# Float32 products of two head pairs in quarters of the array, from the ninth pair on

## The chip, the cores and the metric

One Trainium2 chip, one of its cores. The metric is device time of one execution in microseconds (us), the median of three runs. TensorE is called PE below, its weight loads PEld, VectorE DVE, ScalarE ACT, GpSimdE POOL, and SyncE, which only issues DMAs here, SP.

## The reference

Linear attention on 8 batches of 8 heads (576 tokens, 64 values each), followed by a two-layer MLP on 4608 tokens.

```python
q_s = np.exp(q - np.max(q, axis=-1, keepdims=True))
q_s = q_s / (np.sum(q_s, axis=-1, keepdims=True) + 1e-09)
k_s = np.exp(k - np.max(k, axis=2, keepdims=True))
k_s = k_s / (np.sum(k_s, axis=2, keepdims=True) + 1e-09)
kv = np.einsum('bhsd,bhse->bhde', k_s, v)
attn = np.einsum('bhsd,bhde->bhse', q_s, kv)
x = attn.transpose(0, 2, 1, 3).reshape(4608, 512)
h = x @ w_in                                  # 512 x 2048
g = h * np.tanh(np.log1p(np.exp(h)))          # Mish
out = g @ w_out                               # 2048 x 512
```

All is float32.

## The kernel before

The MLP's matrices are each split into two float32r parts, high and low, and each product is the sum of three float32r matmuls (high by high, high by low, low by high). The tokens go in chunks of 512 (the main part of a batch), and the last 64 tokens of each batch are gathered by way of DRAM (`xt_dram`) into a ninth chunk. A chunk has 16 steps, one for each 128 columns of the hidden layer. A step's `h_mm` makes `ph` from the attention output `xs` (12 matmuls of 512 columns), `act` applies Mish on ACT (`y`) and splits the result on DVE into `gh` and `gl`, and `out_mm`, three steps later, adds it into the four `po` (12 matmuls again). `ph` has two PSUM buffers (`ps_h`), `px` and the other small products two more (`ps_a`), `po` four.

The attention is worked off in the shadow of the MLP, one pair of heads at a time. There are 32 pairs, called items in the code, four for a chunk. Items 0 to 7 and the conversion of the weights stand in a list of tokens written out by hand (`FIRST`); from item 8 (`COLS`) on, `group` writes four MLP steps (`u` = 0 to 3) and puts the steps of one item between them. The order on each engine is the order of these calls. For an item of the later kind:

- k comes transposed (`kt`) for its maxima (`a_kmx`, DVE) and as it is for `a_ksub` (DVE) and the exponential `ke` (`a_exp`, ACT); q likewise: `a_qm` (DVE and POOL), `qe` (ACT), its sums `qs` and `a_qmul` (DVE, POOL), and `a_qt`, which transposes it on DVE into `qT` (512 tokens) and `qTt` (64).
- `a_kv` (step u = 1) multiplies `ke` by v, ten float32 matmuls of 66 columns: the two heads each in one half of the array's columns, five blocks of tokens each. A column of ones in v gives the sums of `ke`.
- `a_ksum` and `a_kvs` (DVE) divide by the sums and write both heads onto the diagonal of `kvbd`, of which two float32r parts `kvr` are made.
- `a_x` (u = 2) multiplies `kvr` by the parts of `qT`: three float32r matmuls of 512 columns in the whole array, into `px`. `a_split` makes the two parts of `xs` from it (ACT and DVE).
- `a_tail1` does the same for the 64 last tokens with one float32 matmul, `pxt`; it stands a group later, right ahead of the next item's `a_kv`. ACT copies it to `xt`, and SP sends it to `xt_dram`.

Of the kernel before, what the change touches and what calls it, by code (L numbers as in the profile page):

```python
# [48 lines left out]
def attn_mish_mlp(ctx: ExitStack, tc: tile.TileContext, q, k, v, wu, qs, kt, out):  # L49
# [39 lines left out]
    kvr = [cp.tile([P, P], F32R, tag=f"kvr{x}", name=f"kvr{x}") for x in "hl"]  # L89
    wi = [cp.tile([P, HP, DFF], F32R, tag=f"wi{x}", name=f"wi{x}") for x in "hl"]  # L90


# [73 lines left out]
    def k_load(i):  # L166
        if i >= NITEM:
            return
        r = at[i] = at.get(i, {})
        t = r["k"] = (pp if i < 3 else lp).tile([P, 2, NC + 1, D], F32, tag=f"k{min(i, 3)}", name=f"k{i}")  # L170
        nc.sync.dma_start(t, k[i])

    def q_load(i):
        if i >= NITEM:
            return
        r = at[i] = at.get(i, {})
        if i >= COLS:
            t = r["q"] = lp.tile([P, NB, 32], F32, tag="q3", name=f"q{i}")
            nc.sync.dma_start(t, qs[i].rearrange("p (n f) -> p n f", f=32))
            t = r["kt"] = lp.tile([P, S], F32, tag="kt", name=f"kt{i}")  # L180
            nc.sync.dma_start(t, kt[i])
# [4 lines left out]
    def a_load(i):  # L186
        q_load(i)
        k_load(i)

    def v_load(i):  # L190
        if i >= NITEM:
            return
        t = at[i]["v"] = vt[min(i, 3)]
        nc.sync.dma_start(t[:, :, :, 0:D], v[i])

    def a_kmx(i):
# [80 lines left out]
    def a_exp(i, which="kq"):  # L277
        if i >= NITEM:
            return
        r = at[i]  # L280
        for nm in which:
            if nm == "q" and i >= COLS:
                e = r["qe"] = ap.tile([P, NB, 32], F32, tag="qe", name=f"qe{i}")
                nc.scalar.activation(e, r["q"], AF.Exp)
                continue
            e = (pp if i in (0, 2) else ap).tile([P, NC + 1, 2, D], F32, tag=f"{nm}e", name=f"{nm}e{i}")
            nc.scalar.activation(e.rearrange("p c h d -> p h c d"), r[nm], AF.Exp)  # L287
            r[nm + "e"] = e

    def a_kv(i):  # L290
        if i >= NITEM:
            return
        r = at[i]
        pkv = psum(i, "o0", f"pkv{i}")
        for c in range(NC + 1):
            if i >= COLS:
                for j in range(2):
                    nc.tensor.matmul(pkv[j * D:(j + 1) * D, 0:D + 2], r["ke"][:, c, j],  # L298
                                     r["v"][:, j, c, :], start=c == 0, stop=c == NC)
            else:  # L300
                nc.tensor.matmul(pkv[:, 0:2 * (D + 2)], r["ke"][:, c].rearrange("p h d -> p (h d)"),
                             r["v"][:, :, c, :], start=c == 0, stop=c == NC)
        r["pkv"] = pkv

# [23 lines left out]
    def a_kvs(i, on_act=False):  # L328
        pkv, rs = at[i]["pkv"], at[i]["rs"]
        bd = kvbd[i in (1, 3) or i >= HP]  # L330
        for j in range(2):
            h = slice(j * D, (j + 1) * D)
            o = 0 if i >= COLS else j * (D + 2)
# [4 lines left out]
        if i >= COLS:  # L338
            nc.vector.tensor_copy(kvr[0], bd)
            sub(nc.vector, kvr[1], bd, kvr[0].bitcast(F32))  # L340

    def a_qt(i):
        if i >= NITEM:
            return
        r = at[i]
        if i >= COLS:
            qe = r["qe"].rearrange("p n f -> p (n f)")
            qT = ap.tile([P, SM], F32, tag="ke", name=f"qT{i}")
            nc.vector.transpose(qT, qe[:, 0:SM])  # L349
            hi = ap.tile([P, SM], F32R, tag="qT", name=f"qTh{i}")  # L350
            nc.scalar.copy(hi, qT)  # L351
            qTt = ap.tile([P, ST], F32, tag="qTt", name=f"qTt{i}")
            nc.vector.transpose(qTt, qe[:, SM:S])
            lo = sp.tile([P, SM], F32R, tag="wc", name=f"qTl{i}")
            sub(nc.vector, lo, qT, hi.bitcast(F32))
            r["qTl"] = lo
            r["qT"] = hi, qTt
# [19 lines left out]
        r["qT"] = qT, qTt  # L377

    def a_x(i):
        if i >= NITEM:  # L380
            return
        b, hp = divmod(i, HP)
        r = at[i]
        qT, qTt = r["qT"]
        px = psum(i, "o3", f"px{i}")
        if i >= COLS:
            nc.tensor.matmul(px, kvr[0], qT, start=True, stop=False)  # L387
            nc.tensor.matmul(px, kvr[1], qT, start=False, stop=False)  # L388
            nc.tensor.matmul(px, kvr[0], r["qTl"], start=False, stop=True)  # L389
        else:  # L390
            nc.tensor.matmul(px, kvbd[i in (1, 3) or i >= HP], qT, start=True, stop=True)
        r["px"] = px
        if i < COLS:
            a_tail1(i)
# [6 lines left out]
    def a_split(i):  # L401
        if i >= NITEM:
            return
        x_hi(i, at[i]["px"])
        x_lo(i, at[i]["px"])


    xt_first = []
# [1 line left out]
    def a_tail2(i):  # L410
        if i < COLS:
            if i == 0:
                xt_first.append(xp.tile([P, 16, ST], F32, tag=f"wo{NF - 1}", name="xt_first"))
            xt = xt_first[0][:, i]
        else:
            xt = ap.tile([P, ST], F32, tag="xt", name=f"xt{i}")
        at[i]["xt"] = xt
        nc.scalar.copy(xt, at[i]["pxt"][:, 0:ST])  # L418

# [42 lines left out]
    def g_mish(n):  # L462
        if not pools:
            ap.tile([P, 36], F32, tag="gap", name="gap")
            start.__exit__(None, None, None)
            pools["wp"] = ctx.enter_context(tc.tile_pool(name="wp", bufs=7))
            pools["rp"] = ctx.enter_context(tc.tile_pool(name="rp", bufs=LAG + 1))
        y = pools["wp"].tile([P, SM], F32, tag="w", name=f"y{n}")
        nc.scalar.activation(y, gs[n], AF.Mish)  # L469
        gs[n] = y  # L470
# [21 lines left out]
                                 stop=f == NF - 1 and i == 2)  # L492

    def evac(c, t, copy):
        ob = pools["wp"].tile([P, DM], F32, tag="w", name=f"ob{c}_{t}")
# [9 lines left out]

    def group(n):
        i = HP + n // G
        for u in range(G):
            m, o = n + u, n + u - LAG
            if m < NSLOT:  # L510
                h_mm(m)
            if u == 0 and NITEM <= i < NITEM + HP:
                t_load(i - NITEM)
            elif u == 1:
                if COLS < i <= NITEM:
                    a_tail1(i - 1)
                if i < NITEM:
                    a_kv(i)
                if COLS < i <= NITEM:
                    a_tail2(i - 1)  # L520
                    a_tail3(i - 1)
                if i < NITEM:
                    a_qsum(i)
                    a_qmul(i)
                    a_ksum(i)
                    a_kvs(i)
                v_load(i + 1)
            elif u == 2:
                a_qt(i)
            if 0 <= o < NSLOT:  # L530
# [6 lines left out]
            if u == 0:  # L537
                a_qm(i + 1)
            if u == 2:
                a_kmx(i + 1)  # L540
                if i < NITEM:
                    a_x(i)
                    a_split(i)
                elif i < NITEM + HP:
                    x_hi(i, tails[i - NITEM])
                    x_lo(i, tails[i - NITEM])
                a_ksub(i + 1)
        a_exp(i + 1)
        a_load(i + 2)
# [56 lines left out]
```

## Time and profile before

| | us |
|---|---|
| median of three runs (lowest, highest) | 883.61 (883.51, 884.49) |
| the profiled execution | 884.14 |
| its span, first to last instruction | 882.4 |
| PE busy | 862.3 |
| DVE busy | 527.6 |
| ACT busy | 318.6 |
| mean granted clock of TensorE | 0.998 |

The profile is of one execution. A record is what one instruction left in it; a float32 matmul leaves two, a float32r matmul one. A record's start is measured, the end of a PE record is modelled, so lengths on PE are read from one start to the next. The timeline view merges like records that follow each other, gives the first start and the last end, and shows those that have started by the window's end and not ended by its start. The chain of waits follows the last instruction back through what released it. Busy times by stage are sums over a stretch of the span.

### The profile page before, as it was taken

The page shows a single profiled execution, that of the slowest core. Times are in us where ns is not written, and L with a number is a line of the kernel's source. Part 1 is how long each engine was busy: PE and PEld are TensorE (multiplying, and loading weights), DVE is VectorE, ACT ScalarE, POOL GpSimd, SP SyncE. Part 2 cuts the span into 40 slices and gives each one's busy share as a digit, 9 for nine tenths or more (in the row PEclk, how much of TensorE's full clock was granted, in tenths as well). Part 3 has the DMA queues.
Part 4 walks back from the last instruction along what each step waited for, and adds up shares of the span by engine and source line. Part 5 has one row for each costly group of instructions (what it writes and reads, how often), then busy time and mean ns, then how long its engine had stood idle before and what let it go on. Part 6 is the DMA issues. An engine that isn't in the chain of part 4 may idle for free.

```text
span 882.4 us, 11236 instructions
## 1 busy us (share of the span) xinstructions
PE 862.3 (98%) x4224; PEld 708.9 (80%) x4224; DVE 527.6 (60%) x1335; ACT 318.6 (36%) x509; POOL 96.3 (11%) x90
## 2 busy tenths in 40 slices
PE   5999999999999999999999999999999999999997
PEld 4777778888888888888888888888888888888886
DVE  8899977666576666666676667665765222222221
ACT  4999772322333333333333323233333111111110
POOL 4333211111111111100011111111110000000000
PEclk9999999999999999999999999999999999999999
DMA  9964342121321123122221132222310020001001
GB/s 312 346 195 136 116 126 63 59 59 59 103 62 58 59 59 107 45 56 59 90 73 38 40 106 59 59 59 70 96 59 14 2 72 13 1 0 48 1 1 48
DMA packets 72822, 66.79 MB, mean 76 GB/s; under 512 B 52800, under 2 KB 52800, under 8 KB 72768
## 3 DMA queue, kind: packets, MB, share of 16 engines
q1 hardware_dynamic: 72448, 65.55, 23.8%
q8 instruction: 33, 0.54, 0.3%
q10 hardware_dynamic: 320, 0.52, 0.2%
q14 instruction: 21, 0.17, 0.1%
HBM read 55.57 MB, written 10.49 MB: 75 GB/s over the span
## 4 chain that ended last, share of the span: by engine, by line
PE 87%; DVE 4%; ACT 4%; DMA 2%; SPq 1%; issue 1%; ACTq 0%
PE po L491 42%; PE ph L449 40%; PE pkv L298 2%; DMA raw_out<-in_w_dram 1%; DMA raw_in<-in_w_dram 1%; DVE wc_out L133 1%; PE px L389 1%; PE px L388 1%; PE px L387 1%; DVE wc_in L133 1%; PE pxt L399 0%; SPq L110 0%; ACT raw_in L121 0%; ACT raw_out L121 0%; SPq L184 0%
## 5 line engine op out<-in xcount | busy, mean ns | idle before, releaser
L491 PE MATMUL po<-wo,gh 128*128 128x512 f32 x1152 | 358.2, 392 | 0.0
L449 PE MATMUL ph<-xs,wih 128*128 128x512 f32 x1152 | 356.8, 391 | 1.1 <-ACT y L469 1.1
L449 PEld LDWEIGHTS ph<-xs,wih 128*128 128x128 f32 x1152 | 214.8, 188 | 45.8 <-ACT y L469 1.9
L491 PEld LDWEIGHTS po<-wo,gh 128*128 128x128 f32 x1152 | 214.2, 188 | 44.8
L449 PE MATMUL ph<-xs,wil 128*128 128x512 f32 x576 | 224.3, 389 | 0.0
L491 PE MATMUL po<-wo,gl 128*128 128x512 f32 x576 | 224.2, 389 | 0.0
L474 DVE CAST gh<-y 128x512 fp32r<-128x512 f32 x130 | 55.4, 426 | 254.1 <-ACT y L469 253.7
L469 ACT ACTIVATE y<-ph 128x512 f32<-128x512 f32 x144 | 86.2, 600 | 225.2 <-PE ph L449 213.0
L491 PEld LDWEIGHTS po<-wo,gl 128*128 128x128 f32 x576 | 108.1, 188 | 22.9
L449 PEld LDWEIGHTS ph<-xs,wil 128*128 128x128 f32 x576 | 108.1, 188 | 22.7
L97 DVE TENSOR_TENSOR gl<-y,gh 128x512 fp32r<-128x512 f32 x144 | 100.2, 697 | 11.5 <-DVE gh L474 0.5
L97 POOL TENSOR_TENSOR q<-q,qm 128x576 f32<-128x576 f32 (+1 forms) x30 | 35.8, 1192 | 466.9 <-DVE qm L225 448.9
L351 ACT CAST qTh<-qT 128x512 fp32r<-128x512 f32 x24 | 14.9, 622 | 89.6 <-DVE qT L349 89.6
L287 ACT ACT_TABLE_LOAD x29 | 37.2, 1283 | 21.0 <-DVE k L275 15.9
L418 ACT COPY xt<-pxt 128x64 f32<-128x64 f32 x24 | 5.1, 213 | 109.5 <-PE pxt L399 109.5
L320 POOL TENSOR_TENSOR qe<-qe,qs 128x576 f32<-128x576 f32 (+1 forms) x28 | 32.9, 1176 | 59.8 <-DVE qs L315 49.2
L469 ACT ACT_TABLE_LOAD x29 | 37.2, 1283 | 0.5
L427 ACT CAST xs<-px 128x512 fp32r<-128x512 f32 x32 | 18.9, 590 | 50.2 <-PE px L389 50.1
L496 DVE COPY ob<-po 128x512 f32<-128x512 f32 x19 | 13.1, 692 | 31.6 <-PE po L491 31.6
L224 DVE COPY sw<-qs 32x18 f32<-32x18 f32 x96 | 26.6, 277 | 1.8
L496 ACT COPY ob<-po 128x512 f32<-128x512 f32 x17 | 10.0, 588 | 47.0 <-PE po L491 40.0
L311 DVE TENSOR_REDUCE qs<-qe 128x18 f32<-128x576 f32 (+1 forms) x32 | 24.5, 764 | 1.7 <-ACT qe L287 1.7
(85 smaller groups left out, 652.8 us busy)
## 6 DMA issues: line engine op xcount, KB each, us to landing
k<-in_k_dram SPq DMA_DIRECT2D x32, 320.0 KB, 3.7
v<-in_v_dram SPq DMA_DIRECT2D x32, 320.0 KB, 3.6
raw_in<-in_w_dram SPq DMA_DIRECT2D x16, 512.0 KB, 6.3
raw_out<-in_w_dram SPq DMA_DIRECT2D x16, 512.0 KB, 4.3
out_dram<-ob SPq DMA_DIRECT2D x32, 256.0 KB, 2.2
q<-in_qs_dram SPq DMA_DIRECT2D x24, 288.0 KB, 2.8
kt<-in_kt_dram SPq DMA_DIRECT2D x24, 288.0 KB, 3.1
q<-in_q_dram SPq DMA_DIRECT2D x8, 320.0 KB, 5.1
```

Of the source, the lines that this page charges most:

```text
L97: eng.tensor_tensor(out, a, b, ALU.subtract)
L133: nc.vector.scalar_tensor_tensor(a, high, 0x80000000, a, ALU.bitwise_and, ALU.bitwise_or)
L224: nc.vector.tensor_copy(sw[32 * (a ^ 1):32 * (a ^ 1) + 32], st[32 * a:32 * a + 32])
L287: nc.scalar.activation(e.rearrange("p c h d -> p h c d"), r[nm], AF.Exp)
L311: nc.vector.tensor_reduce(z, q2, axis=AX.X, op=ALU.add)
L320: eng.tensor_tensor(q2, q2, z.unsqueeze(2).to_broadcast(list(q2.shape)), ALU.mult)
L427: nc.scalar.copy(xs[i][:, 0], src)
L449: nc.tensor.matmul(gs[n], wi[a][:, t, fs], x[:, z], start=t == 0 and i == 0, stop=t == HP - 1 and i == 2)
L469: nc.scalar.activation(y, gs[n], AF.Mish)
L474: copy(hi, gs[n])
L491: nc.tensor.matmul(po[t], g[a][:, t * P:(t + 1) * P], wo[f][:, z], start=f == 0 and i == 0, stop=f == NF - 1 and i == 2)
L496: copy(ob, po[t])
```

## The change

From item 8 on two items are worked on together. A pair of items e, e+1 gets its products in one place, at u = 2 of the odd item's group (`a_pair`): `a_x2` writes four float32 matmuls of 64 columns (tails) and four of 512, each 64 by 64, so each head's product has a quarter of the array to itself; the two heads fed by the upper rows write one PSUM bank and those fed by the lower rows another. The products' results stand in two `ph` buffers (tails) and two `px`. Right behind follows `a_kv2`, the 20 matmuls of `ke` by v of the next two items, into the second of these `ph` buffers. `a_kvs2` divides both items by their sums in one step into `kvt`. The parts `kvr`, `qTh` and `qTl` are gone. The host lays the heads out in another order (`[0, 3, 1, 2]` of four), so that the quarters come out in the right rows.

The steps that feed the pair move: `a_qsum` and `a_qmul` from u = 1 to u = 0, `a_qt` from u = 2 to u = 1; for the odd items `a_kmx`, `a_ksub` and the exponential of k stand at u = 0 and 1 of the group two before their own (`ka`), for the even ones at u = 2, 3 and the group's end (`kb`). Odd items have their own buffers of `ke`, v, `qTt` and `xt`; the pool of `y` has four buffers instead of seven, and the output copies `ob` move to the pool `wc`.

```diff
+    kvt = cp.tile([P, 2, D], F32, tag="kvt", name="kvt")
...
-            if i >= COLS:
-                for j in range(2):
-                    nc.tensor.matmul(pkv[j * D:(j + 1) * D, 0:D + 2], r["ke"][:, c, j],
-                                     r["v"][:, j, c, :], start=c == 0, stop=c == NC)
...
-            nc.vector.tensor_copy(kvr[0], bd)
-            sub(nc.vector, kvr[1], bd, kvr[0].bitcast(F32))
...
-            hi = ap.tile([P, SM], F32R, tag="qT", name=f"qTh{i}")
-            nc.scalar.copy(hi, qT)
...
-            nc.tensor.matmul(px, kvr[0], qT, start=True, stop=False)
-            nc.tensor.matmul(px, kvr[1], qT, start=False, stop=False)
-            nc.tensor.matmul(px, kvr[0], r["qTl"], start=False, stop=True)
...
+    def a_x2(e):
+        r1, r2 = (ps_h.tile([P, 512], F32, tag="h", name=f"pt{e}_{j}") for j in range(2))
+        px = [ps_a.tile([P, 512], F32, tag="a", name=f"px{e + j}") for j in range(2)]
+        pt = r1[:, 0:ST], r2[:, 2 * (D + 2):2 * (D + 2) + ST]
+        for dst, x in ((pt, 1), (px, 0)):
+            for j in range(2):
+                for h in range(2):
+                    a, b = slice(h * D, (h + 1) * D), slice((h ^ j) * D, ((h ^ j) + 1) * D)
+                    nc.tensor.matmul(dst[h][b], kvt[a, j], at[e + j]["qT"][x][a], start=True, stop=True)
+        for j in range(2):
+            at[e + j].update(px=px[j], pxt=pt[j])
+        return r2
+
+    def a_kv2(e, pkv=None):
+        if pkv is None:
+            pkv = ps_h.tile([P, 512], F32, tag="h", name=f"pkv{e}")
+        for i in range(e, e + 2):
+            f = slice((i - e) * (D + 2), (i - e + 1) * (D + 2))
+            for c in range(NC + 1):
+                for j in range(2):
+                    nc.tensor.matmul(pkv[j * D:(j + 1) * D, f], at[i]["ke"][:, c, j], at[i]["v"][:, j, c, :],
+                                     start=c == 0, stop=c == NC)
+        return pkv[:, 0:2 * (D + 2)].rearrange("p (i f) -> p i f", i=2)
+
+    def a_kvs2(e, pkv):
+        rs = ap.tile([P, 2], F32, tag="rs", name=f"rs{e}")
+        nc.vector.tensor_scalar_add(rs, pkv[:, :, D], 1e-9)
+        nc.vector.reciprocal(rs, rs)
+        nc.vector.tensor_tensor(kvt, pkv[:, :, 0:D], rs.unsqueeze(2).to_broadcast([P, 2, D]), ALU.mult)
+
+    def a_pair(e):
+        f = e + 2
+        r2 = a_x2(e) if e >= COLS else None
+        pkv = a_kv2(f, r2) if f < NITEM else None
...
+        ka, kb = (i + 2, NITEM) if i % 2 else (COLS + 1 if i == COLS else NITEM, i + 2)
...
+                if i % 2 and COLS < i < NITEM:
+                    a_pair(i - 1)
+                    v_load(i + 3)
+                    v_load(i + 4)
+                elif i == COLS:
+                    a_pair(i - 2)
```

On PE, in the kernel before, at u = 1 and u = 2 of a group (`pxt` and `pkv` are products of one item, the four `po` and `ph` belong to the MLP):

```order
L399 MATMUL pxt_3120<-qTt_2983,kvbd_90 128x64
L298 MATMUL pkv_3122<-v_102,ke_3057 64x66 x10
L491 MATMUL po_0_2414<-wo_1254,gh_3001 128x512 x2
...
L491 MATMUL po_3_2417<-wo_1371,gl_3055 128x512
L387 MATMUL px_3237<-qTh_3188,kvrh 128x512
L388 MATMUL px_3237<-qTh_3188,kvrl 128x512
L389 MATMUL px_3237<-qTl_3192,kvrh 128x512
L449 MATMUL ph_3245<-xs_2397,wih 128x512 x2
```

`pxt` and `pkv` stand together, `px` two MLP blocks and more behind them, once for each item. On PE, in the changed kernel, at u = 2 of an odd item's group (`pt` are the tails; the `pt_1` of the last two rows is the buffer in which `pkv` is now):

```order
L524 MATMUL po_3_3192<-wo_651,gl_3209 128x512
L391 MATMUL pt_0_3357<-qTt_3090,kvt 64x64
L391 MATMUL pt_1_3358<-qTt_3090,kvt 64x64
L391 MATMUL pt_0_3357<-odd,kvt 64x64
L391 MATMUL pt_1_3358<-odd,kvt 64x64
L391 MATMUL px_3359<-qT_3089,kvt 64x512
L391 MATMUL px_3360<-qT_3089,kvt 64x512
L391 MATMUL px_3359<-qT_3290,kvt 64x512
L391 MATMUL px_3360<-qT_3290,kvt 64x512
L403 MATMUL pt_1_3358<-v_102,ke_3212 64x66 x10
L403 MATMUL pt_1_3358<-v_odd,ke_odd 64x66 x10
L477 MATMUL ph_3406<-xs_2596,wih 128x512 x2
```

All of two items' products now stand in one place, with no MLP matmul between, and the other group of the two has none. On ACT, in the changed kernel, from u = 1 to u = 3 of the same group:

```order
L502 ACTIVATE y_3306<-ph_3277 128x512
L291 ACT_TABLE_LOAD
L291 ACTIVATE ke_odd<-k_3218 128x2x5x64
L502 ACT_TABLE_LOAD
L502 ACTIVATE y_3351<-ph_3326 128x512
L446 COPY xt_3389<-pt_0_3357 128x64
L446 COPY odd<-pt_1_3358 128x64
L455 CAST xs_3394<-px_3359 128x512
L455 CAST xs_3401<-px_3360 128x512
L502 ACTIVATE y_3431<-ph_3406 128x512
```

The exponential of the odd item's k, with a table load ahead of it and one behind, now stands between two Mish in the middle of the group; before, both exponentials of an item stood at the group's end.

## Rows read from the trace of the kernel before

**Rows 1.** The page, busy time of each engine, its share and instructions.

```profile
PE 862.3 (98%) x4224; PEld 708.9 (80%) x4224; DVE 527.6 (60%) x1335; ACT 318.6 (36%) x509; POOL 96.3 (11%) x90
```

**Rows 2.** Busy time by stage: stretch; PE, PEld, DVE, ACT, POOL; clock; DMA.

```profile
137.00:702.00 565.00, 565.00 (x2902) 468.70 (x2902) 363.19 (x1039) 184.20 (x271) 53.41 (x46) 1.00 0.21 63
```

**Rows 3.** Chain of waits, one item: start, length, engine, tile, line, records.

```profile
311.11 0.23 PE px L387
...
311.79 2.72 PE ph L449 x12
...
325.39 0.17 PE pxt L399 x2
325.56 0.73 PE pkv L298 x20
326.29 2.94 PE po L491 x12
...
334.68 0.23 PE px L387
...
335.36 2.72 PE ph L449 x12
```

**Rows 4.** Instructions by line and shape: count, busy us, mean ns, idle before.

```profile
L298 PE MATMUL pkv<-v,ke 128*64 128x66 f32 x480 | 19.3, 227 | 0.0
...
L97 DVE TENSOR_TENSOR qTl<-qT,qTh 128x512 fp32r<-128x512 f32 x24 | 16.6, 692 | 13.5 <-ACT qTh L351 13.5
```

**Rows 5.** Timeline of PE around one `pkv`, in narrow windows: start, length, records.

```profile
325.23 0.22 PE L399 MATMUL pxt<-qTt,kvbd 128*128 128x64 f32 x1
325.29 0.27 PE L399 MATMUL pxt<-qTt,kvbd 128*128 128x64 f32 x1
325.49 0.27 PE L298 MATMUL pkv<-v,ke 128*64 128x66 f32 x1
325.49 0.28 PE L298 MATMUL pkv<-v,ke 128*64 128x66 f32 x2
325.49 0.34 PE L298 MATMUL pkv<-v,ke 128*64 128x66 f32 x4
...
326.07 0.23 PE L298 MATMUL pkv<-v,ke 128*64 128x66 f32 x2
326.22 0.50 PE L491 MATMUL po<-wo,gh 128*128 128x512 f32 x1
```

**Rows 6.** Timeline of PE, one float32 matmul of 512 columns, item 6.

```profile
97.89 0.59 PE L391 MATMUL px<-qT,kvbd 128*128 128x512 f32 x1
...
98.32 0.59 PE L391 MATMUL px<-qT,kvbd 128*128 128x512 f32 x1
```

**Rows 7.** Timeline of ACT at the end of a group; in brackets, idle before.

```profile
341.43 1.28 ACT L287 ACT_TABLE_LOAD   x1 [2.66 <-DVE k L275]
...
343.37 0.67 ACT L284 ACTIVATE qe<-q 128x576 f32<-128x576 f32 x1
...
345.35 0.60 ACT L469 ACTIVATE y<-ph 128x512 f32<-128x512 f32 x1
```

**Rows 8.** Timeline of DVE in the same group and the next.

```profile
328.88 0.70 DVE L349 STREAM_TRANSPOSE qT<-qe 128x512 f32<-128x512 f32 x1
329.51 0.20 DVE L353 STREAM_TRANSPOSE qTt<-qe 128x64 f32<-128x64 f32 x1
...
335.89 0.43 DVE L474 CAST gh<-y 128x512 fp32r<-128x512 f32 x1 [1.16 <-ACT y L469]
...
339.49 0.41 DVE L212 COPY mb<-mb 64x64 f32<-64x64 f32 x2
...
340.54 0.82 DVE L275 TENSOR_TENSOR k<-k,mb 128x640 f32<-128x640 f32 x1
...
348.75 0.75 DVE L311 TENSOR_REDUCE qs<-qe 128x18 f32<-128x576 f32 x1
...
351.15 0.27 DVE L315 RECIPROCAL qs<-qs 128x18 f32<-128x18 f32 x1
```

More of the change, by code (lines that the diff above doesn't have):

```diff
@@ L87, in attn_mish_mlp @@
         nc.vector.memset(t, 0.0)
-    kvr = [cp.tile([P, P], F32R, tag=f"kvr{x}", name=f"kvr{x}") for x in "hl"]
+    kvt = cp.tile([P, 2, D], F32, tag="kvt", name="kvt")
+    ap_odd = cp.tile([P, 2, ST], F32, tag="odd", name="odd")
     wi = [cp.tile([P, HP, DFF], F32R, tag=f"wi{x}", name=f"wi{x}") for x in "hl"]
@@ L169, in k_load, with kt_load @@
         r = at[i] = at.get(i, {})
+        if i >= COLS:
+            kt_load(i)
         t = r["k"] = (pp if i < 3 else lp).tile([P, 2, NC + 1, D], F32, tag=f"k{min(i, 3)}", name=f"k{i}")
         nc.sync.dma_start(t, k[i])
+    def kt_load(i):
+        t = at[i]["kt"] = lp.tile([P, S], F32, tag="kt", name=f"kt{i}")
+        nc.sync.dma_start(t, kt[i])
     def q_load(i):
@@ L179, in q_load @@
             nc.sync.dma_start(t, qs[i].rearrange("p (n f) -> p n f", f=32))
-            t = r["kt"] = lp.tile([P, S], F32, tag="kt", name=f"kt{i}")
-            nc.sync.dma_start(t, kt[i])
             return
@@ L184, in q_load @@
         nc.sync.dma_start(t, q[i])
-    def a_load(i):
-        q_load(i)
-        k_load(i)
     def v_load(i):
@@ L192, in v_load @@
             return
-        t = at[i]["v"] = vt[min(i, 3)]
+        t = at.setdefault(i, {})["v"] = pools["v"] if i > COLS and i % 2 else vt[min(i, 3)]
         nc.sync.dma_start(t[:, :, :, 0:D], v[i])
@@ L285, in a_exp @@
                 continue
-            e = (pp if i in (0, 2) else ap).tile([P, NC + 1, 2, D], F32, tag=f"{nm}e", name=f"{nm}e{i}")
+            if i > COLS and i % 2:
+                e = pools["ke"]
+            else:
+                e = (pp if i in (0, 2) else ap).tile([P, NC + 1, 2, D], F32, tag=f"{nm}e", name=f"{nm}e{i}")
             nc.scalar.activation(e.rearrange("p c h d -> p h c d"), r[nm], AF.Exp)
@@ L295, in a_kv @@
         for c in range(NC + 1):
-            if i >= COLS:
-                for j in range(2):
-                    nc.tensor.matmul(pkv[j * D:(j + 1) * D, 0:D + 2], r["ke"][:, c, j],
-                                     r["v"][:, j, c, :], start=c == 0, stop=c == NC)
-            else:
-                nc.tensor.matmul(pkv[:, 0:2 * (D + 2)], r["ke"][:, c].rearrange("p h d -> p (h d)"),
+            nc.tensor.matmul(pkv[:, 0:2 * (D + 2)], r["ke"][:, c].rearrange("p h d -> p (h d)"),
                              r["v"][:, :, c, :], start=c == 0, stop=c == NC)
@@ L332, in a_kvs @@
             h = slice(j * D, (j + 1) * D)
-            o = 0 if i >= COLS else j * (D + 2)
+            o = j * (D + 2)
             if on_act:
@@ L347, in a_qt @@
             qe = r["qe"].rearrange("p n f -> p (n f)")
-            qT = ap.tile([P, SM], F32, tag="ke", name=f"qT{i}")
+            if i % 2:
+                qT, qTt = sp.tile([P, SM], F32, tag="wc", name=f"qT{i}"), ap_odd[:, 0]
+            else:
+                qT = ap.tile([P, SM], F32, tag="qT", name=f"qT{i}")
+                qTt = ap.tile([P, ST], F32, tag="qTt", name=f"qTt{i}")
             nc.vector.transpose(qT, qe[:, 0:SM])
-            hi = ap.tile([P, SM], F32R, tag="qT", name=f"qTh{i}")
-            nc.scalar.copy(hi, qT)
-            qTt = ap.tile([P, ST], F32, tag="qTt", name=f"qTt{i}")
             nc.vector.transpose(qTt, qe[:, SM:S])
[L354 to L357, printed above, removed]
+            r["qT"] = qT, qTt
             return
@@ L379, in a_x @@
     def a_x(i):
-        if i >= NITEM:
-            return
-        b, hp = divmod(i, HP)
         r = at[i]
-        qT, qTt = r["qT"]
         px = psum(i, "o3", f"px{i}")
-        if i >= COLS:
-            nc.tensor.matmul(px, kvr[0], qT, start=True, stop=False)
-            nc.tensor.matmul(px, kvr[1], qT, start=False, stop=False)
-            nc.tensor.matmul(px, kvr[0], r["qTl"], start=False, stop=True)
-        else:
-            nc.tensor.matmul(px, kvbd[i in (1, 3) or i >= HP], qT, start=True, stop=True)
@@ L392, in a_x @@
-        r["px"] = px
-        if i < COLS:
-            a_tail1(i)
+        nc.tensor.matmul(px, kvbd[i in (1, 3) or i >= HP], r["qT"][0], start=True, stop=True)
+        r["px"] = px
+        a_tail1(i)
+    def a_x2(e):
[10 more added lines that the diff above has]
+        return r2
@@ new lines, in a_kvs2 @@
+    def a_kvs2(e, pkv):
[7 more added lines that the diff above has]
+        pkv = a_kv2(f, r2) if f < NITEM else None
+        if e >= COLS:
+            for j in range(2):
+                a_tail2(e + j)
+                a_tail3(e + j)
+            for j in range(2):
+                x_hi(e + j, at[e + j]["px"])
+                x_lo(e + j, at[e + j]["px"])
+                if j == 0 and pkv is not None:
+                    a_kvs2(f, pkv)
+        elif pkv is not None:
+            a_kvs2(f, pkv)
@@ L399, in a_tail1 @@
         nc.tensor.matmul(px2[:, 0:ST], kvbd[i in (1, 3) or i >= HP], r["qT"][1], start=True, stop=True)
[L401 to L405, printed above, removed]
     xt_first = []
@@ L415, in a_tail2 @@
         else:
-            xt = ap.tile([P, ST], F32, tag="xt", name=f"xt{i}")
+            xt = ap_odd[:, 1] if i % 2 else ap.tile([P, ST], F32, tag="xt", name=f"xt{i}")
         at[i]["xt"] = xt
@@ L465, in g_mish @@
             start.__exit__(None, None, None)
-            pools["wp"] = ctx.enter_context(tc.tile_pool(name="wp", bufs=7))
+            pools["wp"] = ctx.enter_context(tc.tile_pool(name="wp", bufs=4))
             pools["rp"] = ctx.enter_context(tc.tile_pool(name="rp", bufs=LAG + 1))
+            op = ctx.enter_context(tc.tile_pool(name="op", bufs=1))
+            pools["ke"] = op.tile([P, NC + 1, 2, D], F32, tag="ke", name="ke_odd")
+            t = pools["v"] = op.tile([P, 2, NC + 1, D + 2], F32, tag="v", name="v_odd")
+            nc.gpsimd.memset(t[:, :, :, D:D + 2], 1.0)
+            nc.gpsimd.memset(t[ST:P, :, NC, D:D + 2], 0.0)
         y = pools["wp"].tile([P, SM], F32, tag="w", name=f"y{n}")
@@ L494, in evac @@
     def evac(c, t, copy):
-        ob = pools["wp"].tile([P, DM], F32, tag="w", name=f"ob{c}_{t}")
+        ob = sp.tile([P, DM], F32, tag="wc", name=f"ob{c}_{t}")
         copy(ob, po[t])
@@ L511, in group @@
                 h_mm(m)
[L512 to L516, printed above, removed]
-                if i < NITEM:
[L518 to L523, printed above, removed]
+            if u == 0:
+                if NITEM <= i < NITEM + HP:
+                    t_load(i - NITEM)
+                if i == COLS:
+                    v_load(i + 1)
+                a_qsum(i)
+                if i < NITEM:
                     a_qmul(i)
[L525 to L528, printed above, removed]
+            if u == 1:
                 a_qt(i)
+                a_ksub(ka)
             if 0 <= o < NSLOT:
@@ L537, in group @@
             if u == 0:
+                a_kmx(ka)
+            if u == 1:
+                a_exp(ka, "k")
+                if ka < NITEM:
+                    k_load(ka + 1)
                 a_qm(i + 1)
             if u == 2:
[L540 to L544, printed above, removed]
+                if i % 2 and COLS < i < NITEM:
[4 more added lines that the diff above has]
+                    a_pair(i - 2)
+                    v_load(i + 2)
+                    v_load(i + 3)
+                elif NITEM <= i < NITEM + HP:
                     x_hi(i, tails[i - NITEM])
                     x_lo(i, tails[i - NITEM])
-                a_ksub(i + 1)
-        a_exp(i + 1)
-        a_load(i + 2)
+                a_kmx(kb)
+            if u == 3:
+                a_ksub(kb)
+        a_exp(kb, "k")
+        a_exp(i + 1, "q")
+        if kb < NITEM:
+            k_load(kb + 1)
+        q_load(i + 2)
     stages = dict(
@@ L576 @@
     N, SM = B * H // 2, S // 128 * 128
+    q, k, v = (_np.concatenate([x[:2], x[2:].reshape(-1, 4, S, D)[:, [0, 3, 1, 2]].reshape(B - 2, H, S, D)]) for x in (q, k, v))
     def rows(x, n, fill):
```

1 line of the change is left out of this document (removed).

## Prediction, made before the changed kernel was run

> **What bounds the kernel now.** I read the page's busy line first: TensorE (PE) is busy for 862.3 of 882.4 us, VectorE (DVE) for 60% and ScalarE (ACT) for 36% [rows 1]. A busy PE may still be waiting inside its records, so next came the busy time by stage: from 137 to 702 us, where pairs 8 to 31 are worked on, PE is busy all 565 us at a granted clock of 1.00, the upper level of 2.4 GHz, and DVE and ACT have slack [rows 2]. Third, the chain of waits there: it never leaves PE. One pair of heads, called an item below, takes 334.68 - 311.11 = 23.57 us, the same 24 times over. Of this, eight blocks of twelve MLP matmuls (four `ph`, four `po`) take 2.72 us each, 0.227 us a matmul: 21.76 us. What is left is the attention part, 1.81 us an item: `px` three times 0.227 = 0.68; `pxt` 0.17; `pkv` 0.73; and 0.22 by which the `po` block behind `pkv` is longer than the others (2.94) [rows 3]. So the stage pays for whatever PE does, and for nothing on DVE or ACT as long as PE finds its operands ready.
>
> **The MLP part** is left as it is, and so is everything before 137 and after 702 us, but for buffers that change pools. I cost these at nothing: they are reused four steps (over 20 us) later. The work taken from DVE and ACT (of the splits into two float32r parts, 0.69 us for `qTl` alone [rows 4]) gives nothing by itself, since neither ends a wait of PE.
>
> **What goes, for two items:** 2 x 1.81 = 3.62 us of PE.
>
> **What comes.** A float32 matmul leaves two records: 480 for the 240 matmuls of `pkv` [rows 4].
> (a) The 20 `pkv` matmuls stay. Here the trace shows the one thing that matters, two matmuls at once. The timeline cut at 325.49 has one record started, cut at 325.59 two, cut at 325.61 four; the last two start together at 326.07 [rows 5]. The halves of the array (64 columns each) run side by side, in ten steps of (326.07 - 325.60)/8 = 0.059 us, 0.585 us an item. One at a time, twenty records of 0.055 us (the two of `pxt`, nearly as wide, start that far apart [rows 5]) would take 1.1 us. Two items: 1.17 us.
> (b) Changing the array's form. Of the 1.12 us of `pxt`, `pkv` and the longer `po`, 0.585 streams `pkv` and 2 x 0.055 streams `pxt`; 0.43 us is the way into the halves and back. The rows show where: `pkv` starts 0.20 us after the second `pxt` record, and `po` 0.15 after the last `pkv` start, with a first record 0.11 longer than usual [rows 5]. The pair pays the round trip once, not twice: 0.43. New is quarters to halves between `px` and `pkv`, which no row shows; between 0 and a whole round trip of 0.43, I take half, 0.22.
> (c) `px`: four matmuls, each in its own quarter. In the whole array a float32 matmul of 512 columns has its records 98.32 - 97.89 = 0.43 us apart [rows 6], so 0.86 us. If all four run at once that is the price of the four; if none do, it is 3.44. I take 0.86, by the halves, which are the nearest row: there twice the width cost no time.
> (d) The four tails of 64 columns: 2 x 0.055 = 0.11 at once, 0.44 one by one. The first step of `pkv` shows about 0.05 of weight load uncovered, so I take 0.165.
> The sum: 1.17 + 0.43 + 0.22 + 0.86 + 0.165 = 2.85 us, against 3.62: 0.77 saved. Eleven whole pairs: 8.5. Of the twelfth, the first two `pkv` stand alone (1.17 + 0.43 = 1.60) and so do the last two `px` (0.43 + 0.86 + 0.165 = 1.46): 3.06, 0.56 saved. In all 9.0 us. The profiled execution took 884.14 us (882.4 of span and 1.7 around it), 0.5 above the median; the saving is the same from either, so **883.6 - 9.0 = 874.6 us**.
>
> The Trainium skill speaks on (b): "TensorEngine Tiling (Array Packing)", Key Properties, says that changing the tiling mode drains TensorE. By that rule quarters to halves is a full change as well; the entry and exit gaps of [rows 5] agree for whole to half, and the third change at its full 0.43 would make 877.
>
> **What PE may newly wait for.** The order shows that the products take both `ph` buffers, so the second tail needs the Mish of the `ph` block just before; a `po` block of 2.72 us lies between. That Mish stands on ACT behind the exponential of the odd item's k and two table loads. At 341.43 such a row runs from the load, just behind the subtraction of k's maxima on DVE, to the end of the Mish at 345.95; less the exponential of q in it, which is not there now, 4.52 - 0.67 = 3.85 us [rows 7]. The subtraction itself now stands on DVE behind the sums of q (348.75 to 351.42, 2.67), `gh`, `gl` and the maxima of k (335.89 to 339.90, 4.01) and the transposes (0.83), and takes 0.82: 8.3 us after the exponential of q [rows 8]. That one ended at 344.04 [rows 7], 5.96 us after the `ph` block that it follows (338.08 [rows 3]). 5.96 + 8.3 + 3.85 = 18.1 us; PE comes to the products seven blocks or 19.0 us after the same `ph` block. It fits, by some 0.9 us, so I cost it at nothing. Behind the pair stands a `ph` block that needs the first tail's buffer: ACT's short copy of it is hidden by `px` and the `pkv`, 2 us by (a) and (c).
>
> **The rivals.**
> *Quarters of the same rows or of the same output partitions wait for each other.* The halves of [rows 5] share all rows and no output partition; two quarters of one column half do share output partitions, though in different banks, and no row shows that. Then two run at a time: `px` 1.72, tails 0.22, 0.92 more a pair, 12 x 0.92 = 11: **885.6, slower**. It decides from 0.75 us a pair on (9.0/12), where `px` takes over 1.6 us.
> *Staircase.* The second record of a matmul must start before the first of the next, so each quarter overlaps its neighbour alone: five steps in place of two, `px` 5 x 0.43 = 2.15 and tails 0.275, 1.4 more a pair: **891.4**. Against it, in [rows 5] `pkv` starts and ends in twos, where a staircase would start and end with one. With no overlap at all it would be 909 (2.58 + 0.275 a pair). The staircase is what a rule of the Trainium skill gives, "TensorE: Matmul & The Clock Gate", Part 3, The mechanism: matmuls start and end strictly in program order. The twos of the halves don't agree with it if the two records of a matmul stand together in the program.
> *PE waits for a Mish.* The 0.9 us above is an estimate; if it is missed by so much that each pair waits 0.5 us, 12 x 0.5 = 6 us come back: **about 880**. It speaks for this that the measured table load waited 2.66 us for DVE [rows 7]; against it, that half the pairs have no output copies in the group before them, and reach the exponential earlier.
> *The change doesn't do what it says*: the order lists the four tails, four `px` and 20 `pkv` behind each other with no other matmul between, so this has no chance of its own.
>
> **How the numbers follow.** All quarters at once: 0.78. With the third change of form free it is 2.4 us less, with tails also at their least 0.6 more of it: 871.5; with the change in full and tails one by one it is 2.5 + 3.3 us more, 880.4. Its own range of 871.5 to 878 holds it in nine cases of ten. Waits for a Mish: 0.08. Two at a time: 0.07. Staircase or none: 0.07. The range 871.5 to 881 takes the first two and leaves out the last two. A measurement of this kernel can tell about 0.2%, 1.8 us. The first two cases are faster by more; two at a time, at 0.22%, is half same and half slower. Faster 0.86, same 0.04, slower 0.10.
>
> **What would show it.** In the changed trace: the four `px` records start within some 0.02 us of each other and the next four 0.43 later; from the first tail to the next `ph` block 2.7 to 3.0 us; two items take 2 x 21.76 + 2.85 = 46.4 us in place of 47.1; 40 `pkv` records in 1.2 us; PE still busy for the whole stage, with no wait for ACT before the second tail; granted clock still 1.00. Wrong would be `px` records 0.43 us apart one by one or in pairs, or a step from `px` to `pkv` of over 0.5 us.

## The result, and the profile after

The changed kernel took **874.17 us** (median of 4 runs, 873.8 to 874.85), the kernel before 883.72 beside it (4 runs, 883.51 to 884.49): a ratio of 0.9891, 95% interval 0.9874 to 0.9908. It is 9.55 us faster; the prediction said 9.0. The profiled execution took 874.85 us with a span of 873.0, against 884.14 and 882.4 before, so the two traces differ by 9.4 us and can be compared row by row.

First the page's busy line, which answers to [rows 1], then the stage in which the pairs are worked on, from the view of windows (stretch, length; busy time and count of PE, PEld, DVE, ACT, POOL; granted clock; DMA share; GB/s), which answers to [rows 2], then the one line that the view of PE's waits has for that stage (waiting instruction, what it waited for; us in total, times, longest):

```profile
PE 851.9 (98%) x4296; PEld 690.3 (79%) x4296; DVE 480.1 (55%) x1203; ACT 336.2 (39%) x509; POOL 96.4 (11%) x92
...
137.00:690.00 553.00, 551.68 (x2963) 447.63 (x2962) 315.13 (x907) 202.11 (x272) 53.35 (x46) 1.00 0.23 64
...
PE ph L477 <- ACT y L502: 1.3, 1, 1.3
```

PE's busy time fell by 10.4 us and the span by 9.4: about one microsecond of work taken away came back as idle time. The stage shows where. It was busy without a gap before; now 553.00 - 551.68 = 1.3 us is idle, and it is one single wait of a `ph` block for a Mish on ACT. The granted clock is 1.00 as before. DVE's relief (47.5 us less) and ACT's extra work (17.6 us more) don't show in the time.

Now the chain of waits over one whole pair (start, length, what), which answers to [rows 3]:

```profile
305.90 2.72 PE po L524 x12
308.62 0.28 PE pt L391 x8
308.89 0.86 PE px L391 x8
309.75 1.32 PE pt L403 x40
311.07 2.96 PE ph L477 x12
...
354.84 0.28 PE pt L391 x8
```

All of the attention part stands in one burst: tails 0.28, `px` 0.86, the 40 records of `pkv` 1.32 (`pt` L403, for they go into the second tail's buffer), and 2.96 - 2.72 = 0.24 by which the `ph` block behind is longer than the usual 2.72. That is **2.70 us for two items**, where [rows 3] gave 3.62; the same comes from the period, 354.84 - 308.62 = 46.22, less 16 blocks of 2.72. A pair saves 0.92 us.

Whether the quarters run at once is seen in the timeline of PE cut into narrow windows, the way [rows 5] was read. The first row below is what had started by 308.718, the second by 308.740, the third what ran at 309.40 (start of the first, length until the last end, records):

```profile
308.71 0.59 PE L391 MATMUL px<-qT,kvt 64*64 64x512 f32 x1
...
308.71 0.61 PE L391 MATMUL px<-qT,kvt 64*64 64x512 f32 x4
...
309.14 0.61 PE L391 MATMUL px<-qT,kvt 64*64 64x512 f32 x4
```

Four records start within 0.02 us, the next four 0.43 us later, the distance that [rows 6] showed between the two records of one float32 matmul in the whole array. So the products of four heads, two pairs, take together what one float32 product in the whole array takes.

### The profile page after: what moved, and what is told of

Read it like the earlier page. It is cut to its first block, busy times and chain, and to the rows that moved or that the text cites. A ratio compares the mean times of both kernels' runs of the same rounds, so it can differ in the third digit from the quotient of the medians.

```text
span 873.0 us, 11319 instructions
## 1 busy us (share of the span) xinstructions
PE 851.9 (98%) x4296; PEld 690.3 (79%) x4296; DVE 480.1 (55%) x1203; ACT 336.2 (39%) x509; POOL 96.4 (11%) x92
## 4 chain that ended last, share of the span: by engine, by line
PE 86%; ACT 5%; DVE 4%; DMA 2%; SPq 1%; issue 1%; ACTq 0%
PE po L524 41%; PE ph L477 41%; PE pt L403 2%; PE px L391 1%; DMA raw_out<-in_w_dram 1%; DMA raw_in<-in_w_dram 1%; DVE wc_out L134 1%; ACT raw_in L122 1%; DVE wc_in L134 1%; ACT raw_out L122 0%; ACT wc_in L118 0%; DVE wc_out L130 0%; DVE wc_in L130 0%; PE pkv L300 0%; SPq L189 0%
## 5 line engine op out<-in xcount | busy, mean ns | idle before, releaser
L98 DVE TENSOR_TENSOR gl<-y,gh 128x512 fp32r<-128x512 f32 x144 | 104.8, 729 | 12.6 <-DVE gh L507 0.5
L458 DVE TENSOR_TENSOR xs<-px,xs 128x512 fp32r<-128x512 f32 x32 | 21.9, 686 | 34.3 <-ACT xs L455 34.2
L235 DVE TENSOR_REDUCE qm<-q 128x18 f32<-128x576 f32 (+1 forms) x32 | 24.4, 762 | 0.2 <-DMA q<-in_q_dram 0.2
L291 ACT ACTIVATE ke<-k 128x640 f32<-128x640 f32 x20 | 14.8, 742 | 17.9 <-DVE k L276 17.9
L207 DVE STREAM_TRANSPOSE mb<-mxd 32x32 f32<-32x32 f32 x96 | 19.4, 203 | 3.1
```

What stands on the lines that cost most here:

```text
L98: eng.tensor_tensor(out, a, b, ALU.subtract)
L207: nc.vector.transpose(mb[h, h], mxd[h].to_broadcast([32, 32]))
L235: nc.vector.tensor_reduce(qm, qt, axis=AX.X, op=ALU.max)
L458: nc.vector.tensor_tensor(xs[i][:, 1], src, xs[i][:, 0].bitcast(F32), ALU.subtract)
```

## The experiments

The two traces give three terms: (i) four quarters at once, `px` 0.86 a pair; (ii) the burst of 2.70 in place of 3.62 us, 11 times; (iii) the first pair, where PE waits 1.3 us. The runs below test them, all but the repetition of the changed kernel against a rival. All edits are made in the changed kernel, and each alone where nothing else is said.

**The wait at the first pair.** The first `pkv` of the new kind, those of items 8 and 9, stand alone, with no products ahead of them. Here is PE there, and ACT at the same time (start, length, line, instruction; in brackets the idle time before it and what ended it):

```profile
145.82 0.75 PE L403 MATMUL pkv<-v_odd,ke_odd 128*64 128x66 f32 x20
147.89 0.50 PE L477 MATMUL ph<-xs,wih 128*128 128x512 f32 x1 [1.32 <-ACT y L502]
...
145.34 0.58 ACT L529 COPY ob<-po 128x512 f32<-128x512 f32 x1 [0.83 <-PE po L524]
145.95 1.28 ACT L502 ACT_TABLE_LOAD   x1
147.24 0.60 ACT L502 ACTIVATE y<-ph 128x512 f32<-128x512 f32 x1
```

There are two `ph` buffers. `pkv` takes one of them here, so the `ph` block behind it needs the other, whose Mish stands on ACT behind output copies (the last is shown) and a table load of 1.28 us. PE is through with `pkv` at 146.57 and waits until the Mish ends at 147.84. In the later pairs `pkv` goes into the second tail's buffer, and the next `ph` block has the first tail's, which a short copy frees. The edit puts the first `pkv` into the other pool, which is idle then:

```diff
-            pkv = ps_h.tile([P, 512], F32, tag="h", name=f"pkv{e}")
+            pkv = ps_a.tile([P, 512], F32, tag="a", name=f"pkv{e}")
```

> The changed kernel, but the first two pkv (items 8 and 9) go to a buffer of the small products instead of a ph buffer, so that the ph block behind them finds a ph buffer free. Theory (the 1.32 us that PE waits at 147.9 us are for a Mish that stands behind two output copies and a table load): the wait is gone, 1.3 us less, 872.9. Rival (ACT is late for its own reasons, and the next block waits as long): unchanged, 874.2.

Measured 872.96 us (872.8 to 874.55), ratio to the kernel before 0.988 (0.9864 to 0.9897), span 871.0. Both kernels were run again side by side on one chip, since the step is small:

> The kernel whose first pkv go to a buffer of the small products, once more, beside the changed kernel on one chip. Theory: 1.3 us less than the changed kernel, with the wait at the first pair gone. Rival: the two agree within 0.5 us.

> The changed kernel once more, on the same chip and against the same runs of the kernel before: 874.2 by its first runs.

Measured 873.28 (872.93 to 873.67; ratio 0.9876, 0.9861 to 0.989) and 874.46 (874.1 to 874.92; ratio 0.9887, 0.9871 to 0.9904), four runs each, and the slowest of the first is faster than the fastest of the second. The chain of waits with the edit, and the stage in the view of windows:

```profile
144.78 1.32 PE pkv L403 x40
146.09 2.97 PE ph L477 x12
...
137.00:690.00 553.00, 553.00 (x2970) 448.83 (x2969) 314.69 (x905) 201.94 (x272) 53.43 (x46) 1.00 0.23 64
```

The `ph` block follows `pkv` at once, PE is busy for the whole stage, and the two kernels differ by 1.2 us in the runs side by side, as in the first ones (874.17 and 872.96). The wait and its cause are shown: with the buffer elsewhere it is gone and nothing else waits in its place in this stage. This version is the fastest of all that were run.

**One burst or two.** The changed kernel saves partly because products of two kinds stand together. Here, with the other buffer as above, the `pkv` of the next two items are taken out of the burst and put one `po` block later, so that both parts go from whole array to parts and back by themselves:

```diff
-        pkv = a_kv2(f, r2) if f < NITEM else None
+        pkv = a_kv2(f) if e < COLS else None
...
+                if i % 2 and COLS < i < NITEM - 1:
+                    a_kvs2(i + 1, a_kv2(i + 1))
+                    v_load(i + 3)
+                    v_load(i + 4)
```

> The changed kernel, but the 20 pkv of the next two items stand one step later, behind the po block of u = 3, and not right behind the products. Theory (each trip from the whole array to a part and back costs PE its own entry and exit, and standing together saves one): the products alone take 1.34 us as at the last pair, the pkv alone 1.58 (2.91 at the first pair less its wait of 1.32), 2.92 in place of 2.66, eleven times 0.26 = 2.8 us more, less the 1.3 of the first wait that goes too: 875.7. Rival (what counts is the entry alone, the exit is shared with the MLP's own weight load): not over 1.5 us more, 874.4 with the wait gone.

Measured 876.83 us (875.2 to 877.37; ratio 0.9915, 0.99 to 0.993). The runs scatter more than the others, and their median is above both expectations, for a reason that is open; so the verdict rests on the trace, which is of the fastest run (875.2, span 873.4, 2.4 above the version before). The chain of waits, one pair:

```profile
353.71 0.28 PE pt L391 x8
353.99 0.86 PE px L391 x8
354.85 2.95 PE ph L477 x12
...
360.52 1.32 PE pkv L403 x40
...
400.16 0.28 PE pt L391 x8
```

The period is 400.16 - 353.71 = 46.45 us, 0.23 more than in the changed kernel, and 11 x 0.23 = 2.5 is about the difference of the spans; it is near the theory's 2.8 and above the rival's 1.5. The rows also price the parts alone: tails and `px` 0.28 + 0.86 + 0.23 = 1.37, and of the remaining 46.45 - 43.52 = 2.93 for both, `pkv` alone 1.56. Joining them is worth 0.23 us a pair.

**Two more changes of form.** The same price from the other side: the first item's `pkv` is put between the tails and `px`, so that the burst goes quarters, halves, quarters, halves.

```diff
         for dst, x in ((pt, 1), (px, 0)):
+            if between and x == 0:
+                between(r2)
...
-        r2 = a_x2(e) if e >= COLS else None
-        pkv = a_kv2(f, r2) if f < NITEM else None
+            r2 = a_x2(e, lambda r: a_kv2(f, r, (0,)))
+            pkv = a_kv2(f, r2, (1,))
...
```

> The changed kernel with the ten pkv of the first of the next two items moved between the tails and the px, so that the array goes quarters, halves, quarters, halves where it went quarters, halves. Nothing else differs. Theory (a change between quarters and halves costs about 0.15 us each way, by 309.165 + 0.43 to 309.74 in the changed kernel's trace): two changes more, 2.95 in place of 2.66 us a pair, eleven times 0.29 = 3.2 more, 877.4. Rival (the whole round trip's price of 0.43 at each change, as a full drain): 0.86 a pair, 883.6. Rival (a change costs nothing, and what stands there is the weight load of any first matmul): under 0.15 a pair, 875.5.

Measured 878.04 us in a single run, span 876.0. The chain:

```profile
309.61 0.28 PE pt L393 x8
309.88 0.73 PE pt L405 x20
310.62 1.02 PE px L393 x8
311.63 0.73 PE pt L405 x20
312.37 2.93 PE ph L483 x12
...
356.10 0.28 PE pt L393 x8
```

From the first tail to the block behind it takes 2.76 where it took 311.07 - 308.62 = 2.45 in the changed kernel, and the period is 46.49 against 46.22. Eleven times this difference is the 3.0 us by which the span is longer. The 0.27 a pair is near the theory's 0.29 and far from both rivals (0.86, and under 0.15). Two added changes cost 0.3 us: **about 0.15 for one change between quarters and halves**. `px` alone shows it, 1.02 in place of 0.86.

**Two products at once in place of four.** Each product is taken in a half of the array: the head's k-times-v stands in one of two blocks of a table that is zero elsewhere, all 128 rows are summed over, and the heads are put into pairs in another order to match.

```diff
-    kvt = cp.tile([P, 2, D], F32, tag="kvt", name="kvt")
+    kvt = cp.tile([P, 2, P], F32, tag="kvt", name="kvt")
+    nc.vector.memset(kvt, 0.0)
...
-                    nc.tensor.matmul(dst[h][b], kvt[a, j], at[e + j]["qT"][x][a], start=True, stop=True)
+                    nc.tensor.matmul(dst[j][a], kvt[:, j, a], at[e + j]["qT"][x], start=True, stop=True)
...
```

> The changed kernel with the products in halves of the array in place of quarters: all 128 rows, the other head's weights being zeros, two at a time. Everything else stays where it is. Theory (the gain is that four quarters run at once): px takes 4 x 0.43 = 1.72 in place of 0.86, the tails 0.22 in place of 0.11, and the change from quarters to halves (0.15) is gone: 2.66 + 0.86 + 0.11 - 0.15 = 3.48 us a pair, twelve times 0.82 = 9.8 more: 884.0, no better than the kernel before. Rival (the gain is in standing together and in the float32 without splits): under 3 us more, 877.

Measured 884.29 us (883.61 to 885.54), ratio 1.0006 (0.9997 to 1.0016): no change from the kernel before. The chain:

```profile
357.59 0.38 PE pt L392 x8
357.97 1.72 PE px L392 x8
359.69 1.17 PE pt L404 x40
360.86 2.93 PE ph L480 x12
...
404.59 0.38 PE pt L392 x8
```

`px` takes twice 0.86, and the step from `px` to `pkv`, both in halves now, costs nothing: `pkv` 1.17, not 1.32. The period of 47.00 gives 47.00 - 43.52 = 3.48 a pair against 2.70, and all of the gain is gone. This is the price of the prediction's rival in which two run at a time, reached here with all 128 rows in use and not with quarters that wait for each other.

**The order of the quarters.** Two runs change only the order in which the eight products of a burst are written. In the first, the tail and `px` of a quarter stand behind each other, so that four records of one quarter come before the first of the next:

```diff
-        for dst, x in ((pt, 1), (px, 0)):
-            for j in range(2):
-                for h in range(2):
+        for j in range(2):
+            for h in range(2):
+                for dst, x in ((pt, 1), (px, 0)):
```

> The changed kernel with the eight products written quarter by quarter: tail and px of the first quarter, then of the second, and so on, so four records of one quarter stand together ahead of the next quarter's. Theory (each quarter has its own list, and records of other quarters are passed by without limit): still all four at once, 2.66 us a pair, 874.2. Rival (PE looks past only so many records that wait, or only past one): a quarter's first record starts when the one ahead has only its last record left, a staircase, 0.43 us a quarter: 1.3 us a pair more, 889.

Measured 875.5 us in a single run, span 873.4. PE's timeline in narrow windows again (started by 308.765, then running at 309.40; `pt<-odd` are the tails of the odd item):

```profile
308.55 0.28 PE L391 MATMUL pt<-qTt,kvt 64*64 64x64 f32 x2
308.58 0.28 PE L391 MATMUL pt<-odd,kvt 64*64 64x64 f32 x2
...
308.72 0.63 PE L391 MATMUL px<-qT,kvt 64*64 64x512 f32 x4
...
309.15 0.63 PE L391 MATMUL px<-qT,kvt 64*64 64x512 f32 x4
```

The four still start within some 0.04 us. The tails of the odd item start at 308.58, though both `px` of the even item, which start at 308.72, stand ahead of them in the program. So matmuls of other quarters pass one that has not started. If the two records of a matmul stand together in the program, the second record of the first `px`, which starts 0.43 us after the first, is passed in the same way. The period is 46.24, against 46.22. Of what the run lost most lies at the last pair, where PE has to wait for ACT and takes 1.50 us from the first tail to the `ph` block in place of 1.13: its chain has a copy `xt` on ACT there, at 679.79, which the changed kernel's chain doesn't have.

The second run has the loops over j and h the other way round, so that the two quarters fed by the upper rows come first, then the two fed by the lower rows. Before, the first two in the program shared neither rows nor output columns:

```diff
-            for j in range(2):
-                for h in range(2):
+            for h in range(2):
+                for j in range(2):
```

> The changed kernel with the four quarters taken in the other order: both of the upper rows first, then both of the lower rows, so that neighbours in the order share their input rows instead of crossing. Theory (each quarter has its own list, the order does not matter): 2.66 us a pair, 874.2. Rival (quarters that share rows read one after the other when they come next to each other): px starts in twos, up to 0.86 us a pair more, 884.

Measured 875.98 us in a single run, with the span (874.2) 1.2 longer than the changed kernel's. In the chains the first pair starts at 171.15 in place of 169.96, and the last `po` blocks at 857.74 in place of 856.54, 1.2 us later both times: what differs lies ahead of the first pair and isn't the edit's. The burst has the same lengths as in the changed kernel: tails 0.28, `px` 0.86, `pkv` 1.32. In none of the three orders that were run do quarters of the same rows or of the same output columns wait for each other.

**The slack before the second tail.** The prediction costed at nothing the wait for the Mish whose buffer the second tail takes, since one `po` block lies between. Here the burst is put ahead of that `po` block:

```diff
+            early = u == 2 and i % 2 and COLS < i < NITEM
+            if early:
+                act(m)
+                a_pair(i - 1)
+                v_load(i + 3)
+                v_load(i + 4)
...
-            if m < NSLOT:
+            if m < NSLOT and not early:
                 act(m)
...
```

> The changed kernel with each pair one MLP block earlier, right behind the ph block of u = 2 and ahead of the po block that hid that block's Mish. Theory (the second tail waits for this Mish, and the table load of 1.28 us ahead of it starts only when the ph block has ended): PE waits 0.1 + 1.28 + 0.60 + 0.1 = 2.1 us less the first tail's start, some 1.9 us at each of twelve pairs, 23 us more, 897. It also says that the place as it is leaves 2.72 - 2.05 = 0.7 us to spare. Rival (the table is loaded ahead, so that only the Mish of 0.60 is waited for): 0.6 us a pair, 881.

Measured 904.84 us (903.56 to 906.11), two runs, ratio 1.024 (1.0198 to 1.0282): 28.8 us on the spans, some 6 more than expected. The chain at one pair, then at another from the `pkv` on:

```profile
314.07 0.02 issue
...
315.43 0.60 ACT y L502
...
316.08 0.28 PE pt L391 x3
...
317.28 1.32 PE pt L403 x40
318.60 2.96 PE po L524 x12
...
267.45 2.18 PE pt L403 x40
269.63 3.62 PE po L524 x12
```

By the chain PE waits 316.08 - 314.07 = 2.01 us for the Mish, and eleven of the twelve pairs have this wait: without the `po` block in front the wait is real, and the block's 2.72 us covers it by about 0.7. The last pair, whose Mish has no table load ahead of it, waits only 0.73 (from 703.61 to 704.34), so the load's 1.28 us is the difference. The other pair shows the part that was not expected: the same 40 records take 2.18 in place of 1.32. The view of windows (columns as above) over the wait, the burst and the next block, first of this other pair and then of the one shown before it:

```profile
264.00:266.20 2.20, 0.48 (x4) 0.19 (x2) 0.88 (x6) 1.88 (x2) 1.08 (x1) 1.00 0.52 149
266.25:269.60 3.35, 3.35 (x55) 2.41 (x55) 1.10 (x2) 0.21 (x1) 0.03 (x1) 0.71 0.07 15
269.63:272.90 3.27, 3.27 (x13) 2.68 (x13) 1.81 (x5) 1.19 (x3) 0.00 (x0) 0.78 0.36 83
313.70:316.00 2.30, 0.61 (x4) 0.19 (x2) 0.00 (x0) 1.85 (x2) 1.16 (x1) 1.00 0.12 47
316.00:318.60 2.60, 2.52 (x55) 1.65 (x55) 1.12 (x2) 0.24 (x2) 0.00 (x0) 1.00 0.08 19
318.60:321.50 2.90, 2.90 (x13) 2.39 (x14) 1.81 (x5) 1.19 (x3) 0.00 (x0) 1.00 0.16 37
```

After a wait of the same length the granted clock was at the lower of its two levels for a part of the next 6.6 us in one pair (means 0.71 and 0.78) and stayed at 1.00 in the other. Three of the eleven pairs with the long wait show it in this execution. Two bursts lie 48.3 us apart where the clock doesn't fall, 2.1 more than the 46.22 of the changed kernel; each of the three costs 1.5 us beside that. 11 x 2.1 + 0.7 + 3 x 1.5 = 28.3, near the 28.8 measured. Why these three and not the others was not settled.

## Why the prediction was right, and where it was not

**The mechanism holds.** All four quarters run at once, and `px` takes 0.86 us a pair, as term (c) had it. Of the signs named in advance these are there: four starts within 0.02 us, 0.43 to the next four, 46.22 us for two items (46.4), no wait before the second tail, clock at 1.00. Three are there in part. From the first tail to the `ph` block it is 2.45 us, less than the 2.7 to 3.0 that was said; only with the 0.24 inside that block is it 2.70. The 40 `pkv` records read 1.32 in place of 1.2, since that row holds the change from quarters to halves as well; the run in halves, without that change, shows the 1.17 of term (a). And PE is not busy for the whole stage: 1.3 us are idle at the first pair.

**Two rivals are refuted.** Two at a time was made in the run in halves, and it costs about what the rival said: `px` 1.72 and a time of 884.3 (885.6); the changed kernel has neither. The staircase, and with it the rule of the Trainium skill ("TensorE: Matmul & The Clock Gate", Part 3, The mechanism) that matmuls start and end strictly in program order, is not borne out between quarters: in the run by quarters the odd item's tails start at 308.58, ahead of the `px` at 308.72 that stand before them in the program. Within a quarter nothing here speaks against the rule.

**Term (b), the changes of form, was too dear.** It had 0.43 + 0.22 = 0.65; with the other terms as they were, 2.70 - 1.17 - 0.86 - 0.165 = 0.50 was measured. The step from quarters to halves, which no row of before showed and of which half a round trip was taken, costs 0.15 by the added changes. Whole to quarters and halves to whole share the other 0.35, against the 0.43 that was read off [rows 5]. The Trainium skill's rule ("TensorEngine Tiling (Array Packing)", Key Properties) that a change of mode drains the array agrees in so far as each change of form shows a cost; its reading as a third full 0.43 does not. Whether the array drains is not shown. That joining pays once in place of twice was right in size: 3.06 - 2.85 = 0.21 predicted, 0.23 measured.

**The twelfth pair** was put at 1.60 + 1.46 = 3.06 and came to 1.56 + 1.37 = 2.93, by the same term.

**"What PE may newly wait for" missed a wait.** The prediction followed the second tail's buffer and, behind the pair, the first tail's. It took these for all pairs. The first `pkv` of the new kind has no tails ahead of it, takes a `ph` buffer itself, and leaves the next `ph` block the other one, with a Mish behind copies and a table load: 1.3 us. It was not in the sum, and the run with the other buffer gets it back.

**So the total is right by two errors that nearly cancel, which is luck.** 11 x 0.92 + 0.69 = 10.8 us were saved in the pairs, 1.8 more than the 9.0 forecast; 1.3 were lost at the first pair: 9.5 in all, 9.4 on the spans. The version without the loss shows the full saving, 883.83 - 872.96 = 10.9 us against the kernel before in the same comparison.

**The slack was right in size by luck, for another chain sets it.** 0.9 us was said; 0.7 is there (2.72 of the `po` block less 2.01). The estimate added up DVE's way to the odd item's k. ACT's timeline in the changed kernel shows what the Mish waits for in fact:

```profile
302.71 0.74 ACT L291 ACTIVATE ke_odd<-k 128x640 f32<-128x640 f32 x1 [0.26 <-DVE k L276]
305.98 1.28 ACT L502 ACT_TABLE_LOAD   x1 [2.53 <-PE ph L477]
307.27 0.60 ACT L502 ACTIVATE y<-ph 128x512 f32<-128x512 f32 x1
```

The exponential of k is done at 303.45, early. ACT then idles for 2.53 us until PE's `ph` block has ended, and only then loads the table for the Mish: 1.28 + 0.60, and with the ways between the engines 2.0 us. The chain over DVE that the prediction followed ends sooner and decides nothing. In the eleven pairs that have this load it waits for PE's block, with 0.40 to 2.53 us of idle time on ACT ahead of it.

That is not how every load behaves. In the kernel before, a load ahead of a Mish ran while the Mish's input was not there yet, and the Mish waited behind it:

```profile
317.79 1.28 ACT L469 ACT_TABLE_LOAD   x1
319.99 0.60 ACT L469 ACTIVATE y<-ph 128x512 f32<-128x512 f32 x1 [0.91 <-PE ph L449]
```

The difference lies in the program. From 303.5 to 308 us the changed kernel's trace has one more instruction of the Mish's line, a wait (ACTq is ACT's sequencer), right ahead of the load; around 317.79 the kernel before has none:

```profile
L502 ACTq EVENT_SEMAPHORE  x1: 17/17/17, 305.9 to 305.9; - x1
```

In the changed kernel's trace 29 loads for a Mish follow idle time on ACT, and each has such a wait right ahead of it; of the 17 in the kernel before that ran ahead of the Mish's input none has one. What brings the extra wait into the program was not tried.

## What to carry to other kernels

Float32 products over 64 rows and 64 output columns shared the array four at a time here, and four cost what one does. Put them together and beside other work that uses a part of the array, for each change of form costs (here 0.15 us between quarters and halves, 0.35 for the way in and out together). When a change puts a product into a buffer that it shares with another stage, follow that buffer for the first and the last turn of the loop as well as for the middle: the one wait that the new order brought stood at the first turn. And where such a wait would come in a loop that keeps PE full, price it at more than its length, for the clock may fall behind it (here in 3 cases of 11).

## What was not expected of the hardware

- Quarters keep an order each of its own: in the run by quarters the odd item's tails started 0.14 us ahead of the `px` that stand before them in the program, and all four `px` started within 0.04 us.
- A change between quarters and halves costs about 0.15 us, less than half of the 0.43 that the two changes from the whole array to halves and back cost in the kernel before.
- A table load of 1.28 us is hidden by the wait for the Mish's input in the kernel before (0.91 us idle behind the load) and not in the changed kernel (2.53 us idle ahead of it), where the program has an instruction that waits ahead of the load.
- Waits of 2.0 us, once in 48 us of otherwise full work, were followed by the lower granted clock in 3 cases of 11, at about 1.5 us each; behind the one wait of 1.3 us in the changed kernel the clock stayed at 1.00.
